# Letting a quarter of a layer's segment value sums ride in the memory product's unused columns, with layer 1 trailing by one GLU tile

## The chip, the cores and the metric

The kernel runs on one core of a Trainium2 chip. Times are device microseconds of one execution. The kernel before takes 1715.61 us (median of 3 runs, 1714.3 to 1716.24).

The page of a profile names the engines PE (TensorE's matmuls), PEld (its weight loads), DVE (VectorE), ACT (ScalarE), POOL (GpSimd) and SP (SyncE). In the text they have their full names.

## The reference, cut to what matters

Two layers, each a recurrent memory attention (A) followed by a gated linear unit, the GLU (B), over a sequence of 2048 rows of width 448:

```python
x = x + A(layernorm(x));  x = x + B(layernorm(x))    # layer 0
x = x + A(layernorm(x));  x = x + B(layernorm(x))    # layer 1, same weights

def A(x, mem, ...):                 # 64 segments of 32 rows, 8 memory rows
    for s in range(64):
        h = concat(mem, x[segment s])              # 40 rows
        p = softmax(mask(h Wq (h Wk)^T * scale))   # 16 heads
        o = sum over heads of (p (h Wv)) Wo        # 40 rows x 448
        mem = o[:8]                                # needed by the next segment
        outs.append(o[8:])                         # needed only by the GLU
```

The memory rows of a segment need those of the segment before. That is a chain of 64 links per layer. The kernel runs layer 1 four segments behind layer 0, so both layers are in work in the same step.

## The kernel before

Products of weights are folded at the start: `M` holds Wq Wk^T by head, `N` holds Wv Wo by head. A step `t` takes one segment of each layer. In it, `t_unit` multiplies the state by `M` (224 matmuls of 80 columns), scores and softmax follow, and `u_mem` and `u_seg` form "value sums": for every head, the softmax weights times the state. They are stored with the contraction (448 wide, 16 heads) over 56 slabs of 128 partitions. The last product, value sums times `N`, is made at two places.

For the 8 memory rows, at once, because the next step needs them:

```python
# UTm = [128, NO + 1, 16]: 16 columns a slab, 8 for each layer
def un_mem(self, t):
    for k in range(14):
        for j in range(4):
            o = 14 * j + k
            lhs = S.UTm[:, o:o + 2, :]  # 32 columns: this slab's 16 and the next one's 16
            MM(C.b()[32 * j:32 * j + 32, 0:D], lhs, S.N[:, o, :], start=(k == 0), stop=(k == 13))
```

Four tiles of 32 columns run side by side: in the trace their starts are 2 to 18 ns apart and the four take 189 ns together. A tile is 32 wide here and the memory fills 16, so half of each tile computes rows that nobody reads. `hi` and `lo` then hold the result as a sum of two bf16 numbers, and two small products with 0/1 selectors add up the four partial sums (`m_t`, transposed for the next `t_unit`, and `m_nat`, as rows).

For the segment rows, later, once per pair of segments `p`, as 128 columns (2 layers x 2 segments x 32 rows):

```python
def un(self, p):
    if full:      # middle pairs
        for k in range(0, NO, 2):     # 28 pieces of two matmuls for the scheduler
            MM(O.b()[:, 0:D], S.U[:, o, :], S.N[:, o, :], start=(o == 0), stop=(o == NO - 1))   # o = k, k + 1
        XB = O + XA
    else:         # first and last pairs: one layer, 64 columns; two tiles of 64 side by side
        ...
```

Every operation goes to a list scheduler in the program. It fixes each engine's order, picks ScalarE or VectorE for a copy, and assigns the eight PSUM banks. `BIAS` adds a number per kind of operation to its priority. TensorE runs in the order fixed there, so an operation that isn't ready holds up everything after it (a run below starts nothing for 2.86 us for this reason).

## Time and profile before

| | before |
|---|---|
| time | 1715.61 us |
| TensorE, VectorE, ScalarE busy | 98%, 65%, 39% |
| period of four steps (two pairs of segments) | 98.93 us |
| of it matmul stream, by counts and start distances | 94.51 us |
| of it 35 changes of TensorE's tiling, 96 ns each | 3.36 us |
| remainder | 1.06 us |

From the top of the page: busy us, share of the span, and number of instructions.

```profile
PE 1671.6 (98%) x30612; PEld 1228.4 (72%) x30612; DVE 1106.3 (65%) x3157; ACT 670.6 (39%) x1932; POOL 90.7 (5%) x156
```

The groups by shape that the change touches (busy us, mean ns of one | idle before):

```profile
L127 PE MATMUL b<-Nw,big 128*128 128x448 bf16 x1704 | 363.8, 352 | 0.2 <-DVE big L695 0.2
L127 PE MATMUL b<-Nw,UTm 128*32 128x448 bf16 x3752 | 194.0, 359 | 1.5 <-DVE Nw L695 0.8 <-ACT UTm L694 0.6
L127 PE MATMUL b<-Nw,big 128*64 128x448 bf16 x232 | 26.1, 357 | 0.2
```

`Nw,big` is the segments' product (`big` holds `U`), `Nw,UTm` the memory's. The mean of 352 ns is the length of one pipelined matmul, not its cost. The cost is read from starts in the order of time (start us, us, engine, line, operation, out<-in, shapes, count):

```profile
814.21 0.54 PE L127 MATMUL b<-big,hB 128*128 128x448 bf16 x2
814.68 0.39 PE L127 MATMUL b<-PTs,hK 40*128 40x512 bf16 x2
...
820.11 2.83 PE L127 MATMUL b<-Nw,UTm 128*32 128x448 bf16 x56
...
919.04 2.83 PE L127 MATMUL b<-Nw,UTm 128*32 128x448 bf16 x56
```

Two 448-column matmuls take 814.68 - 814.21 = 0.47 us until the next group starts: 189 ns for the first and 285 ns for the second. The second is followed by a change of tiling, from 128x128 to row tiles for 40 rows, and costs 96 ns more. The same 285 ns stand at nearly all such places. The memory's product comes once a step, and the fourth one after that at 820.11 starts at 919.04, which gives the period of 98.93 us. In the middle of the run it repeats to 0.01 us. I call what is left of it after stream and tiling changes the remainder. It holds real waits and small slips at group borders.

The table of TensorE's waits, from 500 to 1300 us, shows one kind of wait above the profile's threshold, once in 98.93 us (us in total, times, longest):

```profile
PE b L127 <- DVE xn L731: 1.6, 8, 0.2
```

So TensorE is fed almost without a gap, and its stream is the bound.

### The profile page before, as it was taken

How to read it: one execution, taken by the hardware profiler on the slowest of the kernel's cores; microseconds unless marked ns; L12 is line 12 of the kernel's file. 1: busy time of each engine (PE TensorE's matmuls, PEld its weight loads, DVE VectorE, ACT ScalarE, POOL GpSimd, SP SyncE). 2: the span in 40 equal slices, each digit the busy share in tenths (PEclk: the TensorE clock that was granted, in tenths of full speed). 3: DMA queues.
4: the chain of work that ended last, by engine and by line, in shares of the span. 5: the costliest groups of instructions: out<-in, count | busy, mean ns of one | idle time of the engine just before them, and what ended most of it. 6: DMA issues, size and time to landing. Idle time of an engine off the chain costs nothing. (4 is left out here: it accounts for less than half of the span.)

```text
span 1712.3 us, 67944 instructions
## 1 busy us (share of the span) xinstructions
PE 1671.6 (98%) x30612; PEld 1228.4 (72%) x30612; DVE 1106.3 (65%) x3157; ACT 670.6 (39%) x1932; POOL 90.7 (5%) x156
## 2 busy tenths in 40 slices
PE   6899999999999999999999999999999999999998
PEld 2567777777777777777777777777777777777765
DVE  8656666666666666666666756566676666567654
ACT  5423433434333344433334444333334443333432
POOL 3000000000000000000000000000000000000000
PEclk9989999999999999999999999999999999999999
DMA  9800000000000000000000000000000000000000
GB/s 228 235 5 4 4 5 4 5 5 5 5 5 5 4 5 6 5 4 5 5 5 4 6 5 4 5 6 5 4 6 5 5 4 6 4 4 4 4 4 5
DMA packets 55760, 27.52 MB, mean 16 GB/s; under 512 B 44584, under 2 KB 54576, under 8 KB 55472
## 3 DMA queue, kind: packets, MB, share of 16 engines
q1 hardware_dynamic: 55120, 22.94, 5.5%
q8 instruction: 241, 3.95, 1.0%
q14 instruction: 47, 0.39, 0.1%
q10 hardware_dynamic: 352, 0.24, 0.1%
HBM read 10.33 MB, written 1.84 MB: 7 GB/s over the span
## 5 line engine op out<-in xcount | busy, mean ns | idle before, releaser
L127 PE MATMUL b<-hT,Mw 128*128 128x80 bf16 (+1 forms) x15232 | 539.6, 200 | 3.4 <-issue 2.3
L127 PEld LDWEIGHTS b<-hT,Mw 128*128 128x128 bf16 x15232 | 534.0, 100 | 11.5 <-issue 3.2
L127 PE MATMUL b<-Nw,big 128*128 128x448 bf16 (+1 forms) x1936 | 389.8, 353 | 0.4 <-DVE big L695 0.2
L695 DVE CAST TTs<-b 128x320 bf16<-128x320 f32 (+5 forms) x565 | 257.5, 456 | 65.7 <-PE b L127 65.3
L127 PEld LDWEIGHTS b<-Nw,big 128*128 128x128 bf16 (+1 forms) x1936 | 161.6, 99 | 133.7 <-issue 12.6
L127 PE MATMUL b<-xBT,big 128*128 128x128 bf16 (+1 forms) x3808 | 208.0, 217 | 1.2 <-ACT xBT L694 0.7
L694 ACT ACTIVATE TTm<-b 64x64 bf16<-64x64 f32 (+4 forms) x319 | 72.1, 226 | 348.3 <-PE b L127 344.3
L127 PEld LDWEIGHTS b<-xBT,big 128*128 128x128 bf16 x3808 | 202.8, 98 | 1.8 <-ACT xBT L694 0.9
L695 DVE CAST TTm<-b 128x80 bf16<-128x80 f32 (+5 forms) x565 | 131.3, 232 | 102.4 <-PE b L127 75.4
L127 PE MATMUL b<-Nw,UTm 128*32 128x448 bf16 x3752 | 194.0, 359 | 1.5 <-DVE Nw L695 0.8
L127 PEld LDWEIGHTS b<-Nw,UTm 128*32 128x32 bf16 x3752 | 100.9, 98 | 86.6 <-ACT UTm L694 13.0
L694 ACT ACTIVATE big<-b 128x512 bf16<-128x512 f32 (+1 forms) x291 | 144.8, 553 | 43.0 <-PE b L127 42.1
L695 POOL COPY hK<-xn 32x448 bf16<-32x448 bf16 x136 | 75.6, 556 | 1512.7 <-DVE xn L731 1465.5
L694 ACT ACTIVATE TTs<-b 64x256 bf16<-64x256 f32 (+4 forms) x319 | 130.8, 410 | 62.5 <-PE b L127 60.0
L695 DVE CAST big<-b 128x512 bf16<-128x512 f32 (+1 forms) x221 | 128.0, 607 | 21.2 <-PE b L127 19.6
L1006 DVE TENSOR_TENSOR hB<-gT,b 128x256 bf16<-128x256 bf16 x226 | 93.8, 416 | 53.3 <-ACT gT L1005 47.1
L1005 ACT ACTIVATE gT<-b 128x256 bf16<-128x256 f32 x226 | 86.1, 381 | 98.7 <-PE b L127 94.3
L909 DVE TENSOR_TENSOR lo<-b,hi 128x448 bf16<-128x448 f32 x67 | 41.5, 619 | 121.7 <-ACT hi L908 121.7
L127 PE MATMUL b<-big,hB 128*128 128x448 bf16 (+1 forms) x476 | 105.8, 355 | 0.0
L908 ACT ACTIVATE hi<-b 128x448 bf16<-128x448 f32 x67 | 36.3, 542 | 128.6 <-PE b L127 128.5
L127 PE MATMUL b<-PTs,hK 40*128 40x512 bf16 (+1 forms) x640 | 84.7, 347 | 1.1 <-ACT PTs L694 0.7
L694 ACT ACTIVATE hT<-b 64x16 bf16<-64x16 f32 (+2 forms) x139 | 25.6, 185 | 124.5 <-DVE hT L695 114.0
(104 smaller groups left out, 1419.9 us busy)
## 6 DMA issues: line engine op xcount, KB each, us to landing
big<-in_A_Wo_dram SPq DMA_DIRECT2D x3, 896.0 KB, 5.5
out_dram<-ys SPq DMA_DIRECT2D x32, 56.0 KB, 1.9
big<-in_B_W_down_dram SPq DMA_DIRECT2D x1, 1568.0 KB, 7.2
XA<-in_A_x_dram SPq DMA_DIRECT2D x28, 56.0 KB, 2.1
big<-in_B_W_up_dram SPq DMA_DIRECT2D x1, 1344.0 KB, 5.9
big<-in_B_W_gate_dram SPq DMA_DIRECT2D x1, 1344.0 KB, 8.8
Nw<-in_A_Wo_dram SPq DMA_DIRECT2D x1, 896.0 KB, 6.7
XA<-in_A_x_dram ACTq DMA_DIRECT2D x4, 56.0 KB, 4.2
```

The source lines that it names most:

```text
L127: ins = E.matmul(out, lhsT=lhsT, rhs=rhs, **kw)
L694: return E.activation(out(), src(), ACT.Copy)
L695: return E.tensor_copy(out(), src())
L908: S.act(lambda E: E.activation(S.hi[:, :], C.b()[:, 0:D], ACT.Copy), D, C.res(), [("hi",)])
L909: S.dve(lambda E: E.tensor_tensor(S.lo[:, :], C.b()[:, 0:D], S.hi[:, :], ALU.subtract), D, C.res() + [("hi",)], [("lo",)])
L1005: S.act(lambda E, k=k, R=R, n=n: E.activation(S.gT[:, k % 2, 0:n], R[0].b()[:, 0:n], ACT.Relu), n, R[0].res(), [("gT", k % 2)])
L1006: S.dve(lambda E, k=k, R=R, n=n, fcs=fcs: E.tensor_tensor(S.hB[:, fcs[0]:fcs[-1] + 1, 0:w], S.gT[:, k % 2, 0:n].rearrange("p (a b) -> p a ...
```

## The change

Intent: fill the 16 useless columns of each memory tile with useful ones. Layer 1's value sums of a pair's first segment (32 rows, a quarter of the pair's 128) are kept in `UTm`. Sixteen ride in the next step's memory product, sixteen in the one after. The selection product `m_nat` gets columns that also pick out the riding rows, and two sums on VectorE add them to the residual. Then `un` has 192 columns left per two pairs: an odd pair makes a full product of 128, an even pair one of 64, as 28 concurrent pairs of halves. The riding rows of a pair are complete only after the next pair has begun, so layer 1's GLU tile comes one pair later. One half tile more stands at the end.

```diff
-        self.UTm = self.sb("UTm", [128, NO + 1, 16])
+        self.UTm = self.sb("UTm", [128, NO, 64])      # 0:16 and 48:64 memory, 16:48 riding
@@ un_mem
-                    lhs = S.UTm[:, o:o + 2, :].rearrange("p a q -> p (a q)")
+                    ... S.UTm[:, o, 32 * w:32 * w + 32]          # w = 1 - t % 2
@@ m_nat
+        p = (t - 2 - w) // 2
+        if p in S.WTILES:
+            r = slice(64, 96)
+            if w == 0:   part[r] = C[r] + XA[r, p % 4]           # VectorE
+            else:        XB[r, (p + 1) % 2] = C[r] + part[r]     # VectorE
@@ u_seg: where layer l's value sums of step t go
+        if l == 0 or p == NP - 1:  return S.U[:, :, 32 * s:32 * s + 32]
+        if s == 0:                 return S.UTm[:, :, 16:48]
+        return S.U[:, :, 64 + 32 * (p % 2):96 + 32 * (p % 2)]
@@ un
-        if r.stop - r.start == 128:
+        if p % 2 and LAG // 2 < p < NSEG // 2:
             ... 56 full matmuls; three sums on VectorE instead of one
         else:
             for k in range(0, NO, 4):    # 14 pieces of four halves
@@ step
+            if last:
+                S.do("ln_b", NP)
+                S.do("b_layer", NP)
@@ BIAS: all priorities retuned
```

Cut here: the selectors in two versions (28 small copies at the start where there were 12), a longer clearing of `UTm`, softmax buffers reused in place to make room.

More of the change, by code (lines that the diff above doesn't have):

```diff
@@ L152 @@
 BIAS = {
-    "b_down": 10000.0, "b_layer": 59336.0, "ln_a": 27598.0, "ln_b": 5000.0, "m_nat": -1055.0, "m_t": 14051.0,
-    "p_t_mem": 31928.0, "s_mem": 11350.0, "s_seg": -1955.0, "seg_pt": 21197.0, "t_unit": 56079.0, "u_mem":
-    29620.0, "u_seg": 10869.0,
+    "b_down": -5000.0, "b_layer": 2000.0, "ln_a": 41619.0, "p_t_mem": 500.0, "s_mem": 74990.0, "s_seg": 72560.0,
+    "seg_pt": -859.0, "u_mem": -38520.0, "u_seg": 2000.0, "un": -37811.0,
 }
@@ L420, in alloc @@
         self.gT = self.sb("gT", [128, 2, 512])
-        self.Sm = self.sb("Sm", [128, 8, KEYS], F32)
         self.Es = self.sb("Es", [128, 8, KEYS], F32)
@@ L425, in alloc @@
         self.Em = self.sb("Em", [128, 2, KEYS], F32)
-        self.Fm = self.sb("Fm", [128, 2, KEYS], F32)
         self.Pm = self.sb("Pm", [128, 128])
         self.PTm = self.sb("PTm", [128, 128])
-        self.UTm = self.sb("UTm", [128, NO + 1, 16])
+        self.UTm = self.sb("UTm", [128, NO, 64])
         self.hi = self.sb("hi", [128, D])
@@ L432, in alloc @@
         self.ident = self.sb("ident", [128, 128])
-        self.selm = self.sb("selm", [128, 16])
-        self.seln = self.sb("seln", [128, 128])
+        self.selm = self.sb("selm", [128, 2, 16])
+        self.seln = self.sb("seln", [128, 2, 128])
         self.maskr = self.sb("maskr", [128, 8 * KEYS])
         self.mTc = self.sb("mTc", [128, 4, MEM])
-        self.mNc = self.sb("mNc", [128, 512])
+        self.mNc = self.ys[:, :, :].rearrange("p a d -> p (a d)")[0:MEM, 0:512]
         self.stat = self.sb("stat", [128, 96], F32)
@@ L440, in alloc @@
         self.cvec = self.sb("cvec", [128, 2], F32)
-        self.csti = self.sb("csti", [128, 128], dt.int32)
+        self.csti = self.gT[:, 0, 0:256].bitcast(dt.int32)
         bank = [self.st.enter_context(self.nc.psum_tensor(f"b{i}", [128, 512], F32)) for i in range(8)]
@@ L547, in setup @@
             S.load_x(p, small)
-        cf = S.Sm[:, :, :].rearrange("p a b -> p (a b)")
-        S.pool(lambda E: E.iota(S.csti[:, :], [[1, 128]], base=0, channel_multiplier=-1), 128, (), [("c", "i")])
+        cf = S.Es[:, :, :].rearrange("p a b -> p (a b)")
+        S.pool(lambda E: E.iota(S.csti, [[1, 128]], base=0, channel_multiplier=-1), 128, (), [("c", "i")])
         S.dve(lambda E: E.memset(S.maskr[:, :], 0.0), 160, (), [("mask", 9)])
-        S.dve(lambda E: E.memset(S.seln[:, :], 0.0), 64, (), [("sel", 9)])
+        S.dve(lambda E: E.memset(S.seln[:, :, :], 0.0), 128, (), [("sel", 9)])
         S.dve(lambda E: E.memset(S.cvec[:, 0:1], EPS), 1, (), [("cvec",)])
         S.pool(lambda E: E.memset(S.XA[64:128, 0:2, :], 0.0), 500, (), [("XA", 0, 1), ("XA", 1, 1)])
-        S.dve(lambda E: E.tensor_copy(cf[:, 0:128], S.csti[:, :]), 128, [("c", "i")], [("Sm",)])
-        S.dve(lambda E: E.tensor_scalar(S.ident[:, :], cf[:, 0:128], 0.0, None, op0=ALU.is_equal), 128, [("Sm",)], [("ident",)])
+        S.dve(lambda E: E.tensor_copy(cf[:, 0:128], S.csti), 128, [("c", "i")], [("Es",)])
+        S.dve(lambda E: E.tensor_scalar(S.ident[:, :], cf[:, 0:128], 0.0, None, op0=ALU.is_equal), 128, [("Es",)], [("ident",)])
         S.pool(lambda E: E.memset(S.M[64:128, 3, 0:28, :], 0.0), 1800, (), [("Mz", 0)])
@@ L564, in setup @@
                 cf[0:32, 0:32].unsqueeze(1).to_broadcast([32, 8, 32]), 0.0, NEG, op0=ALU.is_gt, op1=ALU.mult), 256,
-                [("Sm",), ("mask", 9)], [("mask", j)])
-            S.dve(lambda E, r=r: E.tensor_copy(S.selm[r, :], S.ident[0:32, 0:16]), 16, [("ident",)], [("sel", j)])
-            S.dve(lambda E, r=r: E.tensor_copy(S.seln[r, 32:40], S.ident[0:32, 0:8]), 8, [("ident",), ("sel", 9)], [("sel", j)])
-            S.dve(lambda E, r=r: E.tensor_copy(S.seln[r, 96:104], S.ident[0:32, 8:16]), 8, [("ident",), ("sel", 9)], [("sel", j)])
-        S.pool(lambda E: E.memset(S.UTm[:, :, :], 0.0), 912, (), [("UTm", 0), ("UTm", 1)])
+                [("Es",), ("mask", 9)], [("mask", j)])
+            S.dve(lambda E, r=r: E.tensor_copy(S.selm[r, :, :], S.ident[0:32, 0:32].rearrange("p (w q) -> p w q", w=2)), 32, [("ident",)], [("sel", j)])
+            for w in range(2):
+                for a, m, n in ((32, 16 * w, 8), (96, 16 * w + 8, 8), (64 + 16 * w, 16 * (1 - w), 16)):
+                    S.dve(lambda E, r=r, w=w, a=a, m=m, n=n: E.tensor_copy(S.seln[r, w, a:a + n], S.ident[0:32, m:m + n]), n,
+                          [("ident",), ("sel", 9)], [("sel", j)])
+        S.pool(lambda E: E.memset(S.UTm[:, :, :], 0.0), 3600, (), [("UTm", w, l) for w in range(2) for l in range(2)] + [("UW", c) for c in range(4)])
         S.pool(lambda E: E.memset(S.Pm[:, :], 0.0), 128, (), [("Pm",)])
-        S.pool(lambda E: E.memset(S.XB[64:128, :, :], 0.0), 900, (), [("XB", 0), ("XB", 1)])
+        S.pool(lambda E: E.memset(S.XB[64:128, :, :], 0.0), 900, (), [("XB", i, j) for i in range(2) for j in (1, 2)])
         S.pool(lambda E: E.memset(S.Ps[:, :, :], 0.0), 512, (), [("Ps",)])
@@ L758, in ln_b @@
         S = self
-        S.ln(S.XB[:, p % 2, :], [("XB", p % 2)], 16, "lnB", 1)
+        S.ln(S.XB[:, p % 2, :], [("XB", p % 2, i) for i in range(3)], 16, "lnB", 1)
         T = S.ln_transpose(1, [("xBT",)])
@@ L810, in s_mem @@
         bc = lambda a: st[:, a:a + nl].unsqueeze(2).to_broadcast([128, nl, KEYS])
-        Em, Fm = S.Em[:, 0:nl, :], S.Fm[:, 0:nl, :]
+        Em = S.Em[:, 0:nl, :]
         n = nl * KEYS
@@ L814, in s_mem @@
         S.dve(lambda E: E.tensor_tensor(Em, src(), bc(32), ALU.subtract), n, C.res() + [("sm", 0)], [("Em",)])
-        S.act(lambda E: E.activation(Fm, Em, ACT.Exp, scale=SCALE), n, [("Em",)], [("Fm",)])
-        S.dve(lambda E: E.tensor_reduce(st[:, 34:34 + nl], Fm, AX.X, ALU.add), n, [("Fm",)], [("sm", 1)])
+        S.act(lambda E: E.activation(Em, Em, ACT.Exp, scale=SCALE), n, [], [("Em",)])
+        S.dve(lambda E: E.tensor_reduce(st[:, 34:34 + nl], Em, AX.X, ALU.add), n, [("Em",)], [("sm", 1)])
         S.dve(lambda E: E.reciprocal(st[:, 36:36 + nl], st[:, 34:34 + nl]), nl, [("sm", 1)], [("sm", 2)])
         dst = S.Pm[:, :].rearrange("p (l x) -> p l x", l=2)[:, l0:l1, 0:KEYS]
-        S.dve(lambda E: E.tensor_tensor(dst, Fm, bc(36), ALU.mult), n, [("Fm",), ("sm", 2)], [("Pm",)])
+        S.dve(lambda E: E.tensor_tensor(dst, Em, bc(36), ALU.mult), n, [("Em",), ("sm", 2)], [("Pm",)])
     def s_seg(self, t):
@@ L848, in s_seg @@
         src = lambda: v(G.b()[:, 0:8 * KEYS].rearrange("p (a x) -> p a x", a=8))
-        Sm, Es = v(S.Sm[:, :, :]), v(S.Es[:, :, :])
+        Es = v(S.Es[:, :, :])
         dst = v(S.Ps[:, :, :].rearrange("p a (l x) -> p (a l) x", l=2))[:, :, 0:KEYS]
@@ L853, in s_seg @@
         S.dve(lambda E: E.tensor_tensor(Es, src(), bc(40), ALU.subtract), w, G.res() + [("ss", 0)], [("Es",)])
-        S.act(lambda E: E.activation(Sm, Es, ACT.Exp, scale=SCALE), w, [("Es",)], [("Sm",)])
-        S.dve(lambda E: E.tensor_reduce(st[:, 48:48 + n], Sm, AX.X, ALU.add), w, [("Sm",)], [("ss", 1)])
+        S.act(lambda E: E.activation(Es, Es, ACT.Exp, scale=SCALE), w, [], [("Es",)])
+        S.dve(lambda E: E.tensor_reduce(st[:, 48:48 + n], Es, AX.X, ALU.add), w, [("Es",)], [("ss", 1)])
         S.dve(lambda E: E.reciprocal(st[:, 56:56 + n], st[:, 48:48 + n]), n, [("ss", 1)], [("ss", 2)])
-        S.dve(lambda E: E.tensor_tensor(dst, Sm, bc(56), ALU.mult), w, [("Sm",), ("ss", 2)], [("Ps",)])
+        S.dve(lambda E: E.tensor_tensor(dst, Es, bc(56), ALU.mult), w, [("Es",), ("ss", 2)], [("Ps",)])
     def seg_pt(self, t):
@@ L888, in u_mem @@
              [("PTm",)] + [("hKx", pp, s, l) for l in range(l0, l1)] + [("hKm", pp, s, l) for l in range(l0, l1)],
-             [r for l in C for r in C[l].res()] + [("UTm", l) for l in C], mode=1)
+             [r for l in C for r in C[l].res()] + [("UTm", S.win(t), l) for l in C], mode=1)
         for l in range(l0, l1):
-            S.cp(lambda l=l: S.UTm[:, 0:NO, l * 8:l * 8 + 8], lambda l=l: C[l].b()[:, 0:D].rearrange("p (o q) -> p o q", o=NO), D,
-                 C[l].res(), [("UTm", l)], eng=("act", "dve") if l1 - l0 == 1 else (("act", "dve")[l],))
+            a = 48 * S.win(t) + 8 * l
+            S.cp(lambda a=a: S.UTm[:, :, a:a + 8], lambda l=l: C[l].b()[:, 0:D].rearrange("p (o q) -> p o q", o=NO), D,
+                 C[l].res(), [("UTm", S.win(t), l)], eng=("act", "dve") if l1 - l0 == 1 else (("act", "dve")[l],))
     def un_mem(self, t):
@@ L896, in un_mem @@
         C = S.tile("R", 1)
+        w = S.win(t)
         def mms():
@@ L902, in mms @@
                     o = 14 * j + k
-                    lhs = S.UTm[:, o:o + 2, :].rearrange("p a q -> p (a q)")
-                    out.append(MM(C.b()[32 * j:32 * j + 32, 0:D], lhs, S.N[:, o, :], start=(k == 0), stop=(k == 13)))
+                    out.append(MM(C.b()[32 * j:32 * j + 32, 0:D], S.UTm[:, o, 32 * w:32 * w + 32], S.N[:, o, :], start=(k == 0), stop=(k == 13)))
             return out
-        S.mm(mms, 14 * S.pitch(D) + 100.0, [("UTm", 0), ("UTm", 1)] + (S.Nkeys if t == 0 else []), C.res() + [("hi",), ("lo",)], mode=2)
+        S.mm(mms, 14 * S.pitch(D) + 100.0, [("UTm", w, 0), ("UTm", w, 1)] + [("UW", c) for c in range(4)] + (S.Nkeys if t == 0 else []), C.res() + [("hi",), ("lo",)], mode=2)
         S.act(lambda E: E.activation(S.hi[:, :], C.b()[:, 0:D], ACT.Copy), D, C.res(), [("hi",)])
@@ L919, in m_t @@
         mk = S.mkeys(pp, s, l0, l1)
-        S.mm(lambda: [MM(C.b()[:, c * 16:c * 16 + 16], x[:, w:w + 128], S.selm[:, :], start=(i == 0), stop=(i == 1))
+        S.mm(lambda: [MM(C.b()[:, c * 16:c * 16 + 16], x[:, w:w + 128], S.selm[:, S.win(t), :], start=(i == 0), stop=(i == 1))
                       for c, w in ((0, 0), (1, 128), (2, 256), (3, 320)) for i, x in enumerate((S.hi, S.lo))], 200.0,
@@ L933, in m_nat @@
         C = S.tile("R", 1)
+        w = S.win(t - 1)
         ls = [l for l in range(*S.layers(t)) if not (l == 1 and t == LAG)]
-        S.mm(lambda: [MM(C.b()[:, 0:D], S.seln[:, :], x[:, :], start=(i == 0), stop=(i == 1)) for i, x in enumerate((S.hi, S.lo))],
+        S.mm(lambda: [MM(C.b()[:, 0:D], S.seln[:, w, :], x[:, :], start=(i == 0), stop=(i == 1)) for i, x in enumerate((S.hi, S.lo))],
              2 * S.pitch(D), [("hi",), ("lo",), ("sel",)] + [("sel", j) for j in range(4)], C.res() + [("hKm", pp, s, l) for l in ls])
@@ L939, in m_nat, with win @@
             S.cp(lambda r=r: S.hK[r, pp, s, :], lambda r=r: C.b()[r, 0:D], D, C.res(half=(l,)), [("hKm", pp, s, l)])
+        p = (t - 2 - w) // 2
+        if p in S.WTILES:
+            r = slice(64, 96)
+            if w == 0:
+                S.dve(lambda E: E.tensor_tensor(S.part[r, :], C.b()[r, 0:D], S.XA[r, p % 4, :], ALU.add), D,
+                      C.res(half=(1,)) + [("XA", p % 4, 1)], [("part", 1)])
+            else:
+                S.dve(lambda E: E.tensor_tensor(S.XB[r, (p + 1) % 2, :], C.b()[r, 0:D], S.part[r, :], ALU.add), D,
+                      C.res(half=(1,)) + [("part", 1)], [("XB", (p + 1) % 2, 1)])
+    WTILES = range(LAG // 2, NP - 1)
+    @staticmethod
+    def win(t):
+        return 1 - t % 2
     def u_seg(self, t):
@@ L948, in u_seg @@
             nh = 16 if c < 3 else 8
+            key = {}
+            for l in R:
+                home, k = S.home(t, l)
+                key[l] = home, k + (c,)
             S.mm(lambda c=c, R=R: [m for l in range(l0, l1) for m in S.u_mms(l, c, pp, s, R[l].b(), S.PTs, SEG)],
@@ L951, in u_seg @@
                  [("PTs",)] + [("hKx", pp, s, l) for l in range(l0, l1)] + [("hKm", pp, s, l) for l in range(l0, l1)],
-                 [r for l in R for r in R[l].res()] + [("U", s, l, c) for l in range(l0, l1)] + (S.stage + [("Uz",)] if t == 0 else []), mode=1 if c < 3 else 3)
+                 [r for l in R for r in R[l].res()] + [key[l][1] for l in R] + (S.stage + [("Uz",)] if t == 0 else []), mode=1 if c < 3 else 3)
             for l in range(l0, l1):
-                S.cp(lambda c=c, l=l, nh=nh: S.U[:, c * 16:c * 16 + nh, l * 64 + s * 32:l * 64 + s * 32 + 32],
+                S.cp(lambda l=l, key=key, c=c, nh=nh: key[l][0][:, c * 16:c * 16 + nh, :],
@@ L955, in u_seg, with home @@
                      lambda l=l, nh=nh, R=R: R[l].b()[:, 0:nh * SEG].rearrange("p (u q) -> p u q", u=nh), nh * SEG,
-                     R[l].res(), [("U", s, l, c)])
+                     R[l].res(), [key[l][1]])
+    def home(self, t, l):
+        S = self
+        p, s = t // 2, t % 2
+        if l == 0 or p == NP - 1:
+            return S.U[:, :, 32 * s:32 * s + 32], ("U", s)
+        if s == 0:
+            return S.UTm[:, :, 16:48], ("UW",)
+        return S.U[:, :, 64 + 32 * (p % 2):96 + 32 * (p % 2)], ("U", 2 + p % 2)
@@ L958, in rows, with halves @@
     @staticmethod
     def rows(p):
-        return slice(0, 64) if p < LAG // 2 else slice(64, 128) if p >= NSEG // 2 else slice(0, 128)
-    def halves(self, O, dst, base, base_keys, r, keys):
+        return slice(0, 64) if p <= LAG // 2 else slice(64, 128) if p >= NSEG // 2 else slice(0, 128)
+    def halves(self, O, dst, base, base_keys, r, keys, n=64):
         S = self
-        S.dve(lambda E: E.tensor_tensor(S.part[r, :], O.b()[0:64, 0:D], base, ALU.add), D, O.res(half=(0,)) + base_keys, [("part",)])
-        S.dve(lambda E: E.tensor_tensor(dst, O.b()[64:128, 0:D], S.part[r, :], ALU.add), D, O.res(half=(1,)) + [("part",)], keys)
+        k = ("part", r.start // 64)
+        S.dve(lambda E: E.tensor_tensor(S.part[r, :], O.b()[0:n, 0:D], base, ALU.add), D, O.res(half=(0,)) + base_keys, [k])
+        S.dve(lambda E: E.tensor_tensor(dst, O.b()[64:64 + n, 0:D], S.part[r, :], ALU.add), D, O.res(half=(1,)) + [k], keys)
@@ L969, in un @@
     def un(self, p):
         S = self
-        r = S.rows(p)
         O = S.tile("R", 1)
-        uk = [[("U", s, l, c) for s in range(2) for l in range(2)] for c in range(4)]
-        if r.stop - r.start == 128:
+        XA = lambda r, q: S.XA[r, q % 4, :]
+        XB = lambda r, q: S.XB[r, q % 2, :]
+        lo, x, y = slice(0, 64), slice(64, 96), slice(96, 128)
+        if p % 2 and LAG // 2 < p < NSEG // 2:
             for k in range(0, NO, 2):
                 S.mm(lambda k=k: [MM(O.b()[:, 0:D], S.U[:, o, :], S.N[:, o, :], start=(o == 0), stop=(o == NO - 1)) for o in (k, k + 1)],
-                     2 * S.pitch(D), uk[k // 16], O.res())
-            S.dve(lambda E: E.tensor_tensor(S.XB[:, p % 2, :], O.b()[:, 0:D], S.XA[:, p % 4, :], ALU.add), D,
-                  O.res() + [("XA", p % 4, 0), ("XA", p % 4, 1)], [("XB", p % 2)])
+                     2 * S.pitch(D), [("U", i, k // 16) for i in range(4)], O.res())
+            for src, q, dst, g, half in ((lo, p, lo, p, 0), (x, p - 1, y, p, 1), (y, p, y, p + 1, 1)):
+                S.dve(lambda E, src=src, q=q, dst=dst, g=g: E.tensor_tensor(XB(dst, g), O.b()[src, 0:D], XA(dst, q), ALU.add), D,
+                      O.res(half=(half,)) + [("XA", q % 4, half)], [("XB", g % 2, 2 * half)])
@@ L980, in un @@
         else:
+            u = (2, 3) if p == NSEG // 2 else (0, 1)
             for k in range(0, NO, 4):
-                S.mm(lambda k=k: [MM(O.b()[64 * (o % 2):64 * (o % 2) + 64, 0:D], S.U[:, o, r], S.N[:, o, :], start=(o < 2), stop=(o >= NO - 2))
-                                  for o in range(k, k + 4)], 2 * S.pitch(D), uk[k // 16], O.res(), mode=6)
-            S.halves(O, S.XB[r, p % 2, :], S.XA[r, p % 4, :], [("XA", p % 4, r.start // 64)], r, [("XB", p % 2)])
+                S.mm(lambda k=k: [MM(O.b()[64 * (o % 2):64 * (o % 2) + 64, 0:D], S.U[:, o, 32 * u[0]:32 * u[0] + 64], S.N[:, o, :], start=(o < 2), stop=(o >= NO - 2))
+                                  for o in range(k, k + 4)], 2 * S.pitch(D), [("U", i, k // 16) for i in u], O.res(), mode=6)
@@ L986, in un @@
+            if p < NSEG // 2:
+                S.halves(O, XB(lo, p), XA(lo, p), [("XA", p % 4, 0)], lo, [("XB", p % 2, 0)])
+            elif p == NSEG // 2:
+                S.halves(O, XB(y, p + 1), XA(y, p), [("XA", p % 4, 1)], y, [("XB", (p + 1) % 2, 2)], 32)
+            else:
+                r = slice(64, 128)
+                S.halves(O, XB(r, p + 1), XA(r, p), [("XA", p % 4, 1)], r, [("XB", (p + 1) % 2, i) for i in (1, 2)])
         S.load_x(p + 4)
@@ L1015, in b_layer @@
                  (2 if full else 1) * S.pitch(D), [("hB", k), ("Wd",)], O.res(), mode=0 if full else 6)
-        xb = [("XB", p % 2)]
         if p < NSEG // 2:
             q = p + LAG // 2
+            xb = [("XB", p % 2, 0)]
             if full:
@@ L1023, in b_layer @@
                 S.halves(O, S.XA[64:128, q % 4, :], S.XB[0:64, p % 2, :], xb, r, [("XA", q % 4, 1)])
-        if p >= LAG // 2:
-            q = p - LAG // 2
+        if p > LAG // 2:
+            g = p - 1 - LAG // 2
+            xb = [("XB", p % 2, 1), ("XB", p % 2, 2)]
             if full:
@@ L1030, in b_layer @@
                 S.halves(O, S.ys[64:128, p % 2, :], S.XB[64:128, p % 2, :], xb, r, [("ys", p % 2)])
-            S.qdma(f"ys{p % 2}", lambda E: E.dma_start(S.o_d[64 * q:64 * q + 64, :], S.ys[64:128, p % 2, :]), (), [("ys", p % 2)])
+            S.qdma(f"ys{p % 2}", lambda E: E.dma_start(S.o_d[64 * g:64 * g + 64, :], S.ys[64:128, p % 2, :]), (), [("ys", p % 2)])
     def do(self, name, *args):
```

## The prediction

> **What bounds the kernel now.** The page's busy table gives TensorE 98%, VectorE 65%, ScalarE 39%. The trace's order of time, from 300 to 1600 us, shows matmuls starting without gaps: 448 columns every 189 ns, 128 every 56, 80 every 36, 40 every 25 (the Trainium skill, "TensorE: Matmul & The Clock Gate", "Wait — 56ns, not 53.3ns?", has N/2.4 + about 2.5 ns; this agrees). A pair of 64-column tiles takes about 190 ns together. Where the tiling changes, the next matmul comes 285 ns after a 448-column one: 96 ns per change (the skill, "TensorEngine Tiling (Array Packing)", "Key Properties": changing the mode drains the array). Two pairs of segments (four steps) repeat every 98.93 us; matmul counts times these distances give 94.5 us, 35 mode changes 3.4, which leaves 1.1 us for stalls. TensorE's stream is the bound. The memory recurrence has slack: near the end the state matmuls of successive steps start 16 us apart with one layer (224 x 25 ns in them; with two layers 224 x 36, so I estimate 18.5 to 19), against 24.7 us a step.
>
> **What the change does.**
> - Removes: of 128 value-sum columns, 32 (layer 1's even segment) ride in 16 useless columns of the memory's 32-wide tiles. Even pairs have 64 columns left; their 56 matmuls go as 28 concurrent halves: 28 x 189 = 5.3 us saved per two pairs, 15 times, 79 us. The memory's matmuls and the row selection keep number and size.
> - Adds on TensorE: the halves are another tiling mode, in fragments between other work. The built order has 777 mode changes against 645 (43 against 35 in a steady block of four steps): 132 x 96 ns = 12.7 us. Halves at 190 to 193 ns, and 210 at a fragment's start, cost 3 to 5 us more.
> - Trailing by one GLU tile: pair 2's tile becomes two half tiles, one at the end. Matmul work is equal (64 columns every 29 ns, 128 every 56), plus one layer norm. The tail already waits 3.5 us for its last norm, and the half tile partly fills such waits. Net 0, plus or minus 3 us.
> - Adds on VectorE: seven more sums per two pairs at 0.62 us, about 65 us in all (65% to about 70%). Off the critical path.
> - New dependency: the memory product needs layer 1's value sums of the even segment earlier than `un` did. In the built order their matmuls stand well before it; I expect no long wait.
>
> **On the critical path:** nearly all, because TensorE should stay full. Steady block: 98.9 - 5.3 + 0.8 + 0.3 = 94.7 us. Total: 1715.6 - 79 + 12.7 + 4, edges about -2: 1651 us, range 1638 to 1670; faster by over 2% 0.95, within 2% 0.04, slower 0.01.
>
> **What would show it.** 448-column matmuls of `Nw,big`: 128-wide ones 1704 to 864, 64-wide ones 232 to 1072; a period of four steps near 94.7 us; TensorE still 97 to 98% busy; VectorE near 70%; about 285 ns across the mode changes.
>
> **What would make it wrong.** If the memory product waits for the copies into `UTm`, or the tuned priorities leave stalls before the state matmuls (idle before the `hT,Mw` or `Nw,UTm` groups), the period stays near 96 to 98. If the halves of a fragment do not run concurrently, most of the gain goes. If a step meets the recurrence's length, TensorE idles in the table of waits.

## The result, and the profile after

The changed kernel takes 1662.36 us (median of 4 runs, 1661.61 to 1663.8), the kernel before in the same rounds 1714.95. The ratio is 0.9697 (95% interval 0.968 to 0.9713). Ratios are the mean time of one kernel's runs over that of the other's of the same rounds, so not quite the ratio of the medians quoted. The result is correct.

| | before | predicted | after |
|---|---|---|---|
| time, us | 1715.6 | 1651 (1638 to 1670) | 1662.4 |
| period of four steps, us | 98.93 | 94.7 | 95.44 |
| stream in it | 94.51 | 89.21 | 89.21 |
| tiling changes in it | 35 = 3.36 us | 43 = 4.13 us | 43 = 4.13 us |
| remainder | 1.06 us | 1.4 us | 2.10 us |
| busy TensorE, VectorE | 98%, 65% | 97 to 98%, about 70% | 97%, 69% |

The line of the page that answers the one above:

```profile
PE 1614.9 (97%) x30742; PEld 1192.9 (72%) x30742; DVE 1141.2 (69%) x3172; ACT 717.2 (43%) x2051; POOL 93.3 (6%) x156
```

And the groups by shape:

```profile
L127 PE MATMUL b<-Nw,UTm 128*32 128x448 bf16 x3752 | 193.1, 357 | 2.1 <-DVE UTm L697 1.0 <-ACT UTm L696 0.6
L127 PE MATMUL b<-Nw,big 128*128 128x448 bf16 x864 | 184.8, 353 | 0.0
L127 PE MATMUL b<-Nw,big 128*64 128x448 bf16 x1072 | 123.1, 358 | 0.6 <-DVE big L697 0.5
```

The counts are those predicted. The memory's group kept number and busy time although twice as many of its columns are now read. The halves cost 123.1 us for 1072, which is 115 ns each; the full ones cost 184.8 us for 864, which is 214 each. (The busy times also hold neighbours' overlaps; start to start a pair of halves takes about 190.)

Order of time, the same part of the block. Two memory products, four steps apart, are 936.46 - 841.02 = 95.44 us apart:

```profile
839.56 0.49 PE L127 MATMUL b<-PTm,hK 40*128 40x128 bf16 x10
839.99 1.11 PE L127 MATMUL b<-PTs,hK 40*128 40x512 bf16 x6
841.02 2.83 PE L127 MATMUL b<-Nw,UTm 128*32 128x448 bf16 x56
844.08 0.40 PE L127 MATMUL b<-ident,xn 128*128 128x128 bf16 x4 [0.23 <-DVE xn L733]
844.41 0.30 PE L127 MATMUL b<-PTs,hK 40*64 40x256 bf16 x4
844.64 1.70 PE L127 MATMUL b<-Nw,big 128*64 128x448 bf16 x16
...
936.46 2.83 PE L127 MATMUL b<-Nw,UTm 128*32 128x448 bf16 x56
```

The six `PTs` matmuls should take 3 x 223 ns, and the tiling change after them 96 ns; the group instead lasts 1.03 us until the memory's product, because in its middle it waits for a PSUM bank that ScalarE is still emptying into `UTm`. The table of waits from 500 to 1300 us shows the layer norm twice per block where it showed once (16 waits in place of 8):

```profile
PE b L127 <- DVE xn L733: 3.1, 16, 0.2
```

Most other new waits do not show in that table, because the modelled ends of earlier matmuls cover them. I found them as start distances longer than stream plus tiling change. Per block, from 500 us on, they add up to 1.84 us against 0.79 before: 0.29 and 0.23 before layer norm transposes; 0.27 and 0.17 before value-sum matmuls that wait for a PSUM bank which is still being emptied into `UTm`; 0.23 for `lo`; 0.10 before `xBT` matmuls, whose weight load is released by a copy into `UTm`; 0.12 at the starts of fragments of halves; and smaller ones. Among these the memory product itself waits, at two of its four places, 0.10 and 0.06 us for the copies of the memory's own columns. All but the fragment starts and the smallest sit within some 3 us of a memory product.

Here is one such place, with the other engines:

```profile
864.50 0.61 PE L127 MATMUL b<-PTs,hK 40*128 40x512 bf16 x4
864.60 0.61 DVE L733 TENSOR_SCALAR xn<-XB,stat 128x448 bf16<-128x448 bf16 x2 [0.67 <-ACT stat L730]
864.61 0.54 ACT L912 ACTIVATE hi<-b 128x448 bf16<-128x448 f32 x1
...
865.24 0.69 DVE L697 CAST UTm<-b 128x512 bf16<-128x512 f32 x1
865.27 0.40 PE L127 MATMUL b<-ident,xn 128*128 128x128 bf16 x4 [0.16 <-DVE xn L733]
...
865.85 0.61 DVE L913 TENSOR_TENSOR lo<-b,hi 128x448 bf16<-128x448 f32 x1
...
866.52 0.10 PEld L127 LDWEIGHTS b<-selm,hi 128*128 128x128 bf16 x1 [0.33 <-DVE lo L913]
```

`hi` is ready at 865.15, but VectorE is busy with the norm and then with a copy of value sums, so `lo` is made from 865.85 and TensorE's selection starts at 866.52: its weight load had been idle for 0.33 us and was released by `lo`. VectorE is 69% busy over the run and yet in the way in these two microseconds.

### The profile page after: what moved, and what is told of

It reads as the page before. It is cut to its first block, busy times and chain, and to the rows that moved or that the text cites. A ratio compares the mean times of both kernels' runs of the same rounds, so it can differ in the third digit from the quotient of the medians.

```text
span 1662.0 us, 68199 instructions
## 1 busy us (share of the span) xinstructions
PE 1614.9 (97%) x30742; PEld 1192.9 (72%) x30742; DVE 1141.2 (69%) x3172; ACT 717.2 (43%) x2051; POOL 93.3 (6%) x156
## 3 DMA queue, kind: packets, MB, share of 16 engines
HBM read 10.33 MB, written 1.84 MB: 7 GB/s over the span
## 5 line engine op out<-in xcount | busy, mean ns | idle before, releaser
L127 PE MATMUL b<-Nw,big 128*64 128x448 bf16 (+1 forms) x1936 | 307.8, 355 | 0.6 <-DVE big L697 0.5
L697 DVE CAST TTs<-b 128x320 bf16<-128x320 f32 (+5 forms) x542 | 244.8, 454 | 13.2 <-PE b L127 12.5
L127 PE MATMUL b<-xBT,big 128*128 128x128 bf16 (+1 forms) x3920 | 217.1, 214 | 0.4 <-DVE lo L913 0.4
L127 PEld LDWEIGHTS b<-Nw,big 128*64 128x64 bf16 (+1 forms) x1936 | 128.8, 104 | 105.7 <-issue 14.0
L696 ACT ACTIVATE TTm<-b 64x64 bf16<-64x64 f32 (+5 forms) x338 | 76.7, 227 | 266.7 <-PE b L127 262.7
L696 ACT ACTIVATE TTs<-b 64x256 bf16<-64x256 f32 (+4 forms) x342 | 141.4, 413 | 30.3 <-PE b L127 24.2
L697 DVE CAST TTm<-b 128x80 bf16<-128x80 f32 (+5 forms) x546 | 126.0, 233 | 38.9 <-PE b L127 10.2
L696 ACT ACTIVATE big<-b 128x512 bf16<-128x512 f32 (+1 forms) x242 | 124.5, 555 | 30.7 <-PE b L127 29.9
L697 DVE CAST UTm<-b 128x448 bf16<-128x448 f32 (+2 forms) x124 | 80.2, 647 | 81.0 <-PE b L127 80.1
L697 DVE CAST big<-b 128x512 bf16<-128x512 f32 (+1 forms) x146 | 85.4, 596 | 25.0 <-PE b L127 22.6
L696 ACT ACTIVATE UTm<-b 128x448 bf16<-128x448 f32 (+2 forms) x127 | 64.6, 523 | 24.4 <-PE b L127 23.3
```

The lines of the kernel that those rows point to most:

```text
L127: ins = E.matmul(out, lhsT=lhsT, rhs=rhs, **kw)
L696: return E.activation(out(), src(), ACT.Copy)
L697: return E.tensor_copy(out(), src())
```

## The experiments

The miss to explain is 11 to 12 us: a gain of 64.6 us was predicted, 52.6 came. By the table it is the remainder, 2.10 us against 1.4, about 0.7 us in each of some 15 blocks. Theory V: VectorE's added sums cause it. Rival Q: the new order does, whatever the sums take. A third suspect was the start. In the first trace after, the memory's first product stands at 77.9 us against 73.5.

For every run, the block as read from its trace. Where a period alternates it is the mean. Stream and changes are counted in the built order. In `ride_full_un`, `chunk28`, `chunk56` and `after_oldbias` the remainder also holds stretches in which the granted clock is one half; this comes up below.

| run | time, us | ratio to before | period | stream | changes | remainder |
|---|---|---|---|---|---|---|
| before | 1715.6 | 1 | 98.93 | 94.51 | 35 | 1.06 |
| after | 1662.4 | 0.9697 | 95.44 | 89.21 | 43 | 2.10 |
| `after_again` | 1661.9 | 0.9700 | 95.44 | 89.21 | 43 | 2.10 |
| `setup12` | 1662.5 | 0.9694 | 95.43 | 89.21 | 43 | 2.09 |
| `short_ride_sums` | 1662.4 | 0.9691 | 95.44 | 89.21 | 43 | 2.10 |
| `short_all_sums` | 1661.6 | 0.9695 | 95.44 | 89.21 | 43 | 2.10 |
| `ride_full_un` | 1794.8 | 1.047 | 105.81 | 94.51 | 40 | 7.46 |
| `chunk28` | 1783.2 | 1.0414 | 102.39 | 89.21 | 33 | 10.01 |
| `chunk56` | 1806.7 | 1.0547 | 104.10 | 89.21 | 31 | 11.91 |
| `after_oldbias` | 1749.3 | 1.0215 | 100.69 | 89.21 | 42 | 7.45 |
| `trail_oldbias` | 1725.0 | 1.0082 | 98.92 | 94.51 | 35 | 1.05 |
| `tuned_a` | 1663.7 | 0.9710 | 96.00 | 89.21 | 42 | 2.76 |
| `tuned_b` | 1665.2 | 0.9709 | 95.90 | 89.21 | 43 | 2.56 |
| `before_tuned` | 1699.8 | 0.9917 | 98.15 | 94.51 | 28 | 0.95 |

### The start

```diff
-            for w in range(2):
-                for a, m, n in (...):            # 24 copies of 8 or 16 columns
-                    tensor_copy(S.seln[r, w, a:a + n], S.ident[0:32, m:m + n])
+            tensor_copy(seln[r] viewed [w, a, x][:, :, 1::2, 0:8], ident[0:32, 0:32])     # 4 copies
+            for w in range(2):
+                tensor_copy(S.seln[r, w, 64 + 16 * w:80 + 16 * w], S.ident[...])           # 8 copies
```

> The changed kernel with the row selectors built by 12 copies on VectorE instead of 28 at the start; TensorE's order is identical. In the changed kernel's trace the memory's first product starts at 77.9 us against 73.5 before, and TensorE stands 3.9 us for VectorE's copy of the folded weights while VectorE makes selector copies. Theory S (these copies cost the start): the first product comes 2.5 to 4.5 us earlier and the total falls by as much, to about 1659; the period of four steps stays 95.45 us. Rival (the later start comes from the order of loads or of the fold's own matmuls): first product at 77 to 78 us, total unchanged within 1 us.

Measured: the first product came at 75.3 us, 2.6 earlier, but the total did not move (1662.5 us). Two things speak against theory S. `after_again`, the unaltered kernel, has its first product at 75.8 us, so the start varies by 2 us between executions. And the next four steps take up the difference. Before, the fifth product comes at 73.5 + 79.6 = 153.1 us, after at 77.9 + 77.0 = 154.8, in `after_again` at 75.8 + 77.3 = 153.1, in `setup12` at 75.3 + 78.7 = 154.0. So the start cost between 0 and 2 us of the total in these runs, and the fewer copies gained nothing that can be seen. (The spread is wider still: `short_all_sums`, a run of the next section with the start of the changed kernel, has its fifth product at 157.1.)

What happens there is still instructive. In the first trace after, VectorE is held up by the selector copies and TensorE stands waiting for its copy of a folded weight. In the order of time:

```profile
23.43 4.05 PE L127 MATMUL b<-Nw 128*128 128x448 bf16 x12 [3.91 <-DVE Mw L697]
```

And in the windows of the same trace, from 20 to 32 us (busy us and instructions of TensorE, its weight loads, VectorE, ScalarE and GpSimd, then granted clock, DMA share, GB/s):

```profile
20.00:32.00 12.00, 7.61 (x25) 2.98 (x26) 9.06 (x27) 3.63 (x14) 3.56 (x6) 0.58 1.14 240
```

The clock is granted at 0.58 on average in these 12 us. The trace's clock records put it at one half from 21.9 us on, while TensorE still waits, for 10.2 us.

### VectorE's added sums

```diff
-    tensor_tensor(S.part[r, :], C.b()[r, 0:D], S.XA[r, p % 4, :], ALU.add)
+    tensor_tensor(S.part[r, 0:16], C.b()[r, 0:16], S.XA[r, p % 4, 0:16], ALU.add)
```

The second riding sum is cut alike. The second kernel also cuts two of an odd pair's three sums. What the scheduler is told of their costs is unchanged, so every engine keeps its order. Their outputs are wrong, which doesn't matter for the times.

> The changed kernel with the two sums per pair for the riding rows cut to 16 of 448 columns (wrong values on purpose, same order on every engine). It takes about 1.9 us of VectorE time per four steps away. Theory V (VectorE time of the added sums makes TensorE's added stalls, 1.84 us per four steps against 0.79): stalls fall to 1.2 to 1.5 us, period 95.45 to about 95.0, total about -6 us. Rival Q (the stalls come from how the new order spaces the memory's chain against copies, layer norm and bank releases, whatever the sums take): period 95.3 to 95.45, total -2 us or less.

> As the run with short riding sums, and two of the three sums after an odd pair's product cut to 16 columns too: 6 of the about 7 added sums are nearly free, about 2.8 us of VectorE time per four steps. Theory V: stalls back to about 0.8 to 1.0 us, period about 94.5, total about 1649. Rival Q: period above 95.1, total above 1657.

Measured: the cut sums take 172 to 177 ns in place of 622 to 627 (groups by shape of the changed kernel and of `short_all_sums`, 500 to 1263 us):

```profile
L950 DVE TENSOR_TENSOR part<-b,XA 32x448 f32<-32x448 f32 x16 | 10.0, 622 | 4.4 <-ACT hK L696 4.4
```

```profile
L950 DVE TENSOR_TENSOR part<-b,XA 32x16 f32<-32x16 f32 x16 | 2.8, 172 | 4.4 <-ACT hK L696 4.4
```

The period stayed at 95.44 us and the total at 1662.4 and 1661.6. Every one of the new waits kept its size within 0.01 us. Theory V falls: VectorE time was taken away and TensorE did not notice. In the trace after, the riding sums start some 7 us after a memory product has begun (847.96 after 841.02, 868.92 after 861.73), past the places where TensorE waits.

### The halves undone, and the halves in larger pieces

`ride_full_un` keeps the riding, but an even pair's product is 56 full matmuls again:

```diff
-        if p % 2 and LAG // 2 < p < NSEG // 2:
+        if LAG // 2 < p < NSEG // 2:          # even pairs too; they sum layer 0's rows only
```

> The riding kept, but an even pair's value sums multiplied as 56 full-width matmuls again, not as 28 concurrent halves. Matmul stream by the order and the starts measured before: 1575.0 us and 733 mode changes (70 us), against 1500.8 and 777 (75). Theory H (all of the gain is the halves' concurrency, riding alone only costs): period about 94.5+40x0.096+1.8 = 100.1, total 1728 to 1738, slower than before by about 1%. Rival (riding or the new priorities gain by themselves): at or under 1715.

`chunk28` and `chunk56` change only in how many matmuls the scheduler gets as one piece:

```diff
-            for k in range(0, NO, 4):
+            for k in range(0, NO, 28):        # chunk56: 56
```

> The changed kernel with an even pair's 28 concurrent pairs of halves handed to the scheduler as 2 pieces of 28 matmuls instead of 14 pieces of 4. The matmul stream is the same (1500.8 us); the built order has 600 mode changes instead of 777 (33 instead of 43 in a steady block). Theory M (a mode change costs 96 ns wherever it stands, and the small pieces are not needed as filler): 177 x 96 ns = 17 us less, total 1643 to 1650, period about 94.5 us. Rival F (the small pieces fill waits of the memory's chain): what the changes give back is lost to stalls, period 95.4 or more, total 1658 or more.

> The same in a single piece of 56 matmuls: 565 mode changes, 31 in a steady block. Theory M: 20 us less than the changed kernel, 1640 to 1648, period about 94.3. Rival F: worse than with two pieces, since 5.3 us stand in one lump: period above 96, total above 1665.

Measured: `ride_full_un` is slower than before by 4.7% instead of the expected 1%. The stream went up by the expected 5.3 us a block, and the remainder by another 5.4. The two larger pieces have the full saving in stream and 10 to 12 fewer tiling changes a block, and are 4 to 5% slower than the kernel before. Theory M falls: a change after a 448-column matmul still comes at 285 ns, but larger pieces lose far more than the changes cost, at least in this order. Neither kernel's priorities were retuned for its larger pieces, so what such pieces cost in an order made for them is not shown. Rival F was right, and I had underrated it by far (it said "1658 or more").

The longest loss is one wait per block for the segment's softmax (in `chunk28` 22.9 of the 49.9 us that TensorE's table of waits holds from 500 to 1263.5 us; the rest are waits of up to 1.0 us). It is seen in `chunk28` (order of time):

```profile
843.46 0.30 PE L127 MATMUL b<-maskr,ident 128*128 128x320 bf16 x1 [0.61 <-DVE TTm L697]
843.59 0.96 PE L127 MATMUL b<-hT,TTs 128*128 128x40 bf16 x32
844.39 0.35 PE L127 MATMUL b<-hT,TTm 128*128 128x40 bf16 x8
847.60 0.40 PE L127 MATMUL b<-ident,Ps 128*128 128x128 bf16 x4 [2.86 <-DVE Ps L859]
```

In the changed kernel, small pieces of the segments' product or of the GLU stand between the scores and the softmax's transposes. Here nothing is left to stand there. `ride_full_un` has the same wait, although its pieces are small; a likely reason is that the priorities had been tuned for other work, but no run retunes them.

```profile
838.20 0.35 PE L127 MATMUL b<-hT,TTm 128*128 128x40 bf16 x8
841.36 0.61 PE L127 MATMUL b<-ident,Ps 128*128 128x128 bf16 x4 [2.80 <-DVE Ps L859]
```

And the wait costs more than itself. These are `ride_full_un`'s windows around it (columns as above):

```profile
835.00:840.00 5.00, 3.55 (x93) 2.88 (x90) 3.55 (x11) 3.05 (x12) 0.00 (x0) 1.00 0.06 16
840.00:847.00 7.00, 5.64 (x50) 4.13 (x51) 4.39 (x13) 3.74 (x10) 0.00 (x0) 0.54 0.00 1
```

The granted clock drops to one half for 6.8 us in every block. By the trace's clock records the drop comes at 840.6, 0.8 us before the wait ends. They show 13 such windows, 105.8 us apart. Stream and tiling changes do not grow in that time, so the remainder does: start distances of `xBT` matmuls in the slow stretch (107 ns in place of 56) alone account for 1.5 us of the 7.46.

So `ride_full_un` does not isolate the value of the halves as I had wanted. That rests on counts and start distances: 5.3 us less stream in the block.

### Parts of the change: priorities, trailing

`after_oldbias` is the changed kernel with the `BIAS` of before. `trail_oldbias` is the trailing alone: all value sums go to `U` as before, nothing rides, middle pairs are 56 full matmuls, and layer 1's sums go to the next tile.

```diff
@@ trail_oldbias, home()
-        if s == 0:
-            return S.UTm[:, :, 16:48], ("UW",)
-        return S.U[:, :, 64 + 32 * (p % 2):96 + 32 * (p % 2)], ("U", 2 + p % 2)
+        return S.U[:, :, 64 * l + 32 * s:64 * l + 32 * s + 32], ("U", 2 * l + s)
```

> The changed kernel with the priorities of the kernel before. Stream the same, 763 mode changes against 777. If the retuned priorities are needed to keep TensorE full (theory P), the stalls of 1.84 us per four steps rise to 3 us or more and the total to 1680 to 1715, which eats a third or more of the gain. If not, the total stays within 8 us of 1662.

> The trailing alone: layer 1's tile goes through the GLU one pair later, nothing rides, every middle pair's value sums are one full-width product as before; priorities of the kernel before. By the order: stream 1580.3 us and 646 mode changes, against 1579.8 and 645. If trailing is free, as predicted (net 0, plus or minus 3 us), the total is 1712 to 1720 and the period 98.9 to 99.3. If the extra half tile and layer norm are exposed at the end, the total is 1721 to 1726, with the period unchanged.

Measured: with the old priorities the same change is not a gain but a loss of 2% (1749.3 us, remainder 7.45). Theory P holds, more strongly than I had put it: not a third of the gain is eaten but all of it. TensorE then waits longer (us in total from 500 to 1263.5 us, times, longest):

```profile
PE b L127 <- DVE UTm L698: 11.4, 8, 1.4
PE b L127 <- ACT hK L697: 9.5, 8, 1.2
```

Part of its remainder is clock here too: from 500 to 1300 us, about eight blocks, the clock records show six half-rate windows, 27.2 us in all. I estimate from this that at most 1.7 of the 7.45 us a block is lost to it.

The trailing alone, with old priorities, cost 12.6 us (1725.0 against 1712.4 of the same rounds), with the period unchanged. The end explains most of it: from the last memory product to the end of the span it takes 47.6 us against 39.6, and the step before that 19.8 against 17.0. (Its fifth product also comes 2.4 us later, within the spread of starts seen above.) The changed kernel has 39.2 at the end: with the retuned priorities, matmuls of the tile before fill the waits of the last one's norm. `after_oldbias`, which differs from it in the priorities alone, has 48.7. So trailing is free only in an order made for it.

### The order alone

A theory remained: the changed kernel's order leaves slack, and a better one would bring the missing 11 us. I let the program's own scheduler evaluate some thousands of priority sets and took two that it held to be clearly shorter, and one for the kernel before. Apart from `BIAS`, these three kernels have one rule more, a bonus for operations of the tiling that TensorE is in:

```diff
-                t, o = max((x for x in lst if x[0] <= lim), key=lambda x: (x[1].prio, -x[0]))
+                keep = BIAS.get("keep", 0.0) if e == "pe" else 0.0
+                t, o = max((x for x in lst if x[0] <= lim),
+                           key=lambda x: (x[1].prio + (keep if x[1].mode == mode else 0.0), -x[0]))
```

> The changed kernel, with 12 selector copies at the start and other priorities (found by trying some thousands of sets in the program's own scheduler). The work is the same: 30742 matmuls, stream 1500.8 us, 771 mode changes against 777, same sums on VectorE. Only the order differs, and which engine takes a copy. Theory Q (the miss of the prediction, about 11 us, is stalls that the changed kernel's order leaves, 1.84 us per four steps): stalls fall to about 1 us or less, period 94.0 to 94.6, total 1647 to 1655. Rival (the added work itself or its mode changes cost them, in any order): period 95.2 or more, total 1659 or more.

> A second, very different set of priorities for the same kernel, 786 mode changes. Theory Q: also 1647 to 1656, period 94.0 to 94.7. Rival: 1659 or more. If one of the two orders is faster and the other not, the order's detail on the chip decides, and the scheduler's view of it is not enough.

> The changed kernel unaltered, to stand on the same chip as the two reordered ones: 1660 to 1664, period 95.44, as before.

> The kernel before, with priorities sought in the same way: 532 mode changes against 645 (28 against 35 in a steady block), stream the same 1579.8 us. If the change's gain were mostly a better order, this kernel would come near 1662. I expect 113 x 96 ns = 11 us less at most and no gain from stalls, which are 0.8 us per four steps already: 1701 to 1710, period 98.2 to 98.5.

Measured: both reorderings are as fast as the changed kernel and no faster (ratios 0.9710 and 0.9709 against 0.9700, all intervals about plus or minus 0.002). Their remainders are 2.76 and 2.56 us, not about 1. The waits sit at other places but are of the same kinds, as the table of waits of `tuned_b` shows (500 to 1263 us, eight blocks):

```profile
PE b L127 <- DVE xn L735: 3.8, 16, 0.7
PE b L127 <- ACT UTm L698: 3.3, 8, 0.4
PE b L127 <- DVE Ps L861: 2.7, 8, 0.3
```

In the steady middle both are slower than the changed kernel (1152.0 and 1151.6 us over twelve blocks against 1145.3); they gain this back at the two ends. Theory Q in the form in which I put it (a better order brings the stalls to 1 us) is not confirmed. Nor is its rival, since neither of two orders can show that all orders do this. The scheduler's view of what is ready when is not exact enough to settle a tenth of a microsecond per place.

`before_tuned` took 1699.8 us against 1713.6 in the same rounds, 0.8% better than the kernel before and a little better than the 1701 to 1710 that I expected. Its period fell by 0.78 us, of which seven fewer tiling changes are 0.67. So the kernel before could gain from a better order too. Against that kernel the changed one still has 0.970 / 0.9917 = 0.978 of the time. The change is worth about 2% where both are ordered with like care, and 3% as it was made.

No correct run beats the changed kernel by more than the noise.

## Why the prediction was right, and where it missed

1662.4 us lies in the range of 1638 to 1670, and "faster by over 2%" came true. The gain was 52.6 us where 64.6 were predicted. (One detail of its first paragraph: N/2.4 + 2.5 fits the measured 448, 128 and 80 columns; for 40 columns it alone would give 19 ns, and the trace has 25.)

- **The stream** was right: 28 x 189 ns = 5.3 us less in a block, and the counts of full and half matmuls were exactly those forecast. Read so, the block is 98.93 - 5.30 + 0.77 + 1.04 = 95.44.
- **The tiling changes** were right: 43 against 35 in a block, at 96 ns each. The built order gave their number, the trace before their price.
- **The mis-sized term is the stalls.** The prediction allowed 0.3 us more a block (fragment starts) and "no long wait". No wait is long, but many short ones came: the remainder rose by 1.04 us, from 1.06 to 2.10. At 0.74 us too little in about 15 blocks, that is the 11 us. What the prediction listed as its first danger, that the memory product waits for copies into `UTm`, is a small part of it: 0.10 and 0.06 us at two of four products. The larger waits at `UTm` (0.27 + 0.17 us a block) come a step earlier, where value-sum matmuls wait for a PSUM bank, and the prediction did not name those.
- **"Off the critical path" for the added VectorE sums** was right, and is the point best shown: cutting six of the seven changed nothing. Their size was not: VectorE's busy time rose by 35 us, not 65, and ScalarE's by 47, because the scheduler, which picks the engine of a copy, gave more copies to ScalarE.
- **Trailing, "net 0"**: true of the changed kernel (the tail is 39.2 us against 39.6), but only because the priorities were retuned. Alone, with the old ones, it cost 12.6 us. The prediction's reason (the half tile fills a wait) holds only in an order that does fill it (with the old priorities the changed kernel's tail is 48.7).
- **Concurrency in fragments** held: the halves ran in pairs.
- **The recurrence's slack**: a full step with both layers never met its length. The steady steps are 20.7 to 27.4 us long, and their product was not delayed by more than some tenths of a microsecond.

Shown: the miss is in stalls between matmuls, not in stream, tiling changes or the added sums, and the size of such stalls depends on the order, from 2.1 to 11.9 us a block for the same matmuls, half-rate stretches included. Open: what keeps it at 2 us or more. Candidates are VectorE's and ScalarE's queues in the few microseconds around a memory product, and the eight PSUM banks. The trace shows waits of both kinds, and no run separates them.

## What to carry to other kernels

For an engine that is fed without gaps, cost a change by counting what it issues, times start distances from the trace, and add its mode changes; that part came out exact. Then allow for stalls: what remains after stream and mode changes doubled here, and went up sevenfold, half-rate stretches included, with priorities tuned for other work. (That less movable work was left to cover the same waits is the likely reason; no run isolates it.) In an order made for small pieces, keep movable work in small pieces even where that costs mode changes, and retune the order with the change before judging it.

## What the Trainium skill lacked or had wrong

- "TensorEngine Tiling (Array Packing)", "Key Properties", says that changing the mode drains the array, but gives no price. Here a 448-column matmul is followed after 285 ns instead of 189: 96 ns per change, 43 times in 95.44 us.
- "TensorE: Matmul & The Clock Gate", "What's actually happening", has the clock fall to one half after an idle window of about 3.4 us, and its table "Why this matters for your kernels" warns of gaps over about 3 us. Here less was enough. In `ride_full_un` one wait of 2.80 us, once in 105.8 us, brought a half-rate window of 6.8 us each time. In `after_oldbias` no wait is longer than 1.4 us from 500 to 1300 us, and six half-rate windows came, each at the second of two waits of 1.2 and 1.4 us or up to 1.1 us after it. In the 3.4 us before each of these windows TensorE was busy for 1.3 to 1.7 us by the profile's modelled ends. That the granted values are one half or full, and whole windows are multiples of 3.4 us, agrees. `chunk28` and `ride_full_un` ran at a mean granted clock of 0.968 and 0.970 against 0.994.
- The rule in "Perfetto Trace Analysis", "Identifying the Most-Contended Engine", that a busy TensorE says little about the distance to the roofline, agrees: it reads 98% before and 97% after, although the same useful work takes 3% less time. The page calls the weight loads' busy share a good measure instead. It is no better here: 72% before and 72% after. In `chunk28`, which is 7% slower than the changed kernel, both fall alike, to 92% and 68%. Start distances told more than both.
